# A third float64 load buffer with a changed scheduler, and five small edits, in an attention and two-MoE kernel

## The chip, the cores and the metric

The kernel runs on one core of one Trainium2 chip. The metric is the device time of one execution in microseconds, the median of several runs. The engines that matter are TensorE (PE, with its weight loads as PEld), VectorE (DVE), ScalarE (ACT) and the DMA queue that SyncE (SP) issues.

## The reference

A sigmoid attention over 4 batches and 12 heads of 448 tokens gives 1792 tokens of width 768. Two feed-forward layers follow, one after the other, each with a hidden width of 2048. The weights `w_in` and `w_out` come as float64 and are read as pairs of 32-bit words.

```python
scores = scale * np.matmul(q, k.transpose(0, 1, 3, 2)) - np.log(S)
attn = 1.0 / (1.0 + np.exp(-scores))
x = np.matmul(attn, v)                      # then (B*S, H*D) = (1792, 768)
# layer 1
r = np.maximum(x @ w_in, 0.0)
x = (s * (r * r) + b) @ w_out
# layer 2
h = x @ w_in
x = (np.maximum(h, 0.0) + alpha * np.minimum(h, 0.0)) @ w_out
```

## The kernel before

**Matmuls.** Every product of the two layers is made by the seven products M1 to M7 of the Strassen-Winograd scheme, and each operand is split in a high part (a CAST on ACT, L450) and a low part (a subtraction on DVE, L453). A term is three matmuls of 128x448: high times low (L547), high times high (L548), low times high (L549). The low part of a weight is thus needed at the third matmul. A "mp" is a pair of 128-row blocks of the hidden width; there are 8 in each phase, and one takes 63 matmuls, 9 for each of M1 to M7.

**Stages on PE.** Attention runs to 135.59 us of the span. Then come four pairs of phases: the tokens are halved, and each half goes through `w_in` and `w_out` of a layer. The first of them, `first_phase`, runs from 135.59 to 244.69 us and takes its weights straight from the buffers in which they are made; the later ones read them back from DRAM. The order of the products in `first_phase` is M1, M5, M6, M2, M4, M7, M3 (in mp7 M2 stands before M6). M1 and M2 share a bank of PSUM, M5 and M4 another, M6 and M7 a third: M2 can begin when M1's bank has been copied out (L558, ACT), M4 when M5's has been added (L568, DVE), M7 when M6's has been.

**Weights.** `quad` (L335) makes the operands of one mp: two loads of 768 KB on SP into the buffers `r640` and `r641` (shown as `r`; L328), for each of them a Prelu on ACT over the high words (L362), a TENSOR_SCALAR (L365) and a SCALAR_TENSOR_TENSOR (L370) on DVE, then four DVE subtractions or additions (L383), which leave seven blocks in `quada`, `quadb` or `quadc`. SP stores the blocks to DRAM (L402, L411). `first_phase` splits the blocks of `quadb` (even mp) and `quada` (odd mp) into the ring `rinq0` to `rinq3`: the first entry holds M1 and M5, the second M6 and M2, the third M4 and M7, the fourth M3. The buffers that `unit` (L426) loads weights back into, `raw0` and `raw1`, lie in the same memory as `quadb`.

**Results of M1 to M7.** They are gathered in `g`: M1 is copied (L558), M5 and M6 added (L568), M2 copied, M7 added and subtracted (L568, L576), M3 added. Relu (L594), Square (L629) and Identity with scale s and offset b (L632) then go over all four blocks of a mp, 1792 elements, on ACT.

**Order.** No engine chooses at run time. `Plan` collects every operation with an estimated duration and its dependencies; `place` puts, again and again, the operation that can start first (at equal starts the one with the least spare time, `late`) on its engine. That order is written out; each engine and the SP queue then run their rows strictly in this order. `order` repeats this ROUNDS times.

Of the kernel before, what the change touches and what calls it, by code (L numbers as in the profile page):

```python
# [16 lines left out]
P = 128  # L17
NWARM = 6
CELL = 64
QUEUES = {"SP": 0.07, "POOL": 1.0}  # L20
AHEAD = 1.0
ROUNDS = 3
SAFE = 0.0
PIPE = {"DVE": 0.08, "ACT": 0.09}
EARLY = 7
# [29 lines left out]
class Plan:  # L55
# [57 lines left out]
    def place(self, succ, late, pe):  # L113
        n = len(self.ops)
        share = self.shared()
        wrote, used = ([{} for _ in share] for _ in range(2))

        def behind(i, eng):

            x = 0.0  # L120
            for mine, of in zip(self.uses[i], (wrote, used)):
                for t in mine:
                    for o in share[t]:
                        for e, at in of[o].items():
                            if at > x and e != eng:
                                x = at
            return x
        left = [len(op[3]) for op in self.ops]
        est = [0.0] * n
        pe_at = 0  # L130
        open_ = {}
        for i in range(n):
            if left[i] == 0:
                open_.setdefault(self.ops[i][0], set()).add(i)
        free, done, at = {}, [], {}
        pipe = 0.0
        while len(done) < n:
            best = None
            for eng, cand in open_.items():
                if not cand:  # L140
                    continue
                f = free.get(eng, 0.0)
                if eng in QUEUES:
                    f = max(f, pipe - AHEAD)
                if eng == "PE":
                    i = pe[pe_at]
                    if i not in cand:
                        continue
                    est[i] = max(est[i], behind(i, eng))
                    pick = (max(f, est[i]), late[i], i)  # L150
                else:
                    while True:
# [3 lines left out]
                        if x <= pick[0]:  # L156
                            break
                        est[i] = x
                if best is None or pick < best[0]:
                    best = (pick, eng)  # L160
            (start, _, i), eng = best
            open_[eng].discard(i)
            if eng == "PE":
                pe_at += 1
            dur, lat = self.ops[i][1:3]
            if eng in QUEUES:
                free[eng] = start + QUEUES[eng]
                pipe = max(pipe, start) + dur
                end = pipe
            else:  # L170
                end = free[eng] = start + dur
            at[i] = start
            done.append(i)
            for k, mine in enumerate(self.uses[i]):
                for t in mine:
                    for of in (used, wrote)[: k + 1]:
# [33 lines left out]
def tile_kernel(  # L210
# [3 lines left out]
    vt: bass.AP,  # L214
    w_in1: bass.AP,
    w_out1: bass.AP,
    s: bass.AP,
    b: bass.AP,
    w_in2: bass.AP,
    w_out2: bass.AP,  # L220
    alpha: bass.AP,
    out: bass.AP,
):
    nc = tc.nc
# [16 lines left out]

    NSLOT = 37
    NRING, NRAW, NTMP = 3, 2, 7
    UNIT = 8 * P
    WQ = KH * P
    base0 = -(-nc.sbuf_base // (4 * CELL)) * CELL
# [16 lines left out]
    def own(name, n):  # L263
# [1 line left out]

    SLOTS = take(NSLOT * SLOT)
    RING0 = take(NRING * 2 * UNIT)
    PROD = take(8 * WQ + 7 * WQ)
    SPARE = take(NRAW * UNIT + 7 * WQ)
    RING = [tensor(f"ring{i}", RING0 + i * 2 * UNIT, 2 * UNIT, F32R) for i in range(NRING)]  # L270
    RING4 = [tensor(f"rinq{i}", RING0 + i * 4 * WQ, 4 * WQ, F32R) for i in range(4)]
# [8 lines left out]
        [(tensor("xraw12", MID + 2 * SLOT + XB, XB), 0, XB)],  # L280
        [(tensor("xraw13", MID + XB, S), 0, S), (tensor("xraw14", NEG.base, 2 * S), S, XB)],
    ]
    R64 = [tensor(f"r64{i}", PROD + 4 * WQ * i, 4 * WQ) for i in range(2)]
    QUADS = [
        tensor("quada", PROD + 8 * WQ, 7 * WQ),
        tensor("quadb", SPARE, 7 * WQ),
        tensor("quadc", NEG.base, 7 * WQ),
    ]
    TMP = [own(f"tmp{i}", S) for i in range(NTMP)]
    SMALL = take(CELL)  # L290
    BIAS, SC, BC, WARM, AL, NAL = (
        tensor(x, SMALL + at, n)
        for x, at, n in (
            ("bias", 0, 1), ("sc", 8, 1), ("bc", 16, 1), ("warm", 24, 1), ("al", 32, NFC), ("nal", 48, NFC)
        )
    )
    IDLE = tensor("idle", TMP[0].base, P)
# [14 lines left out]
        return 0.08 + 0.53e-3 * n  # L312

    def dma_t(n):
        return n * 4 * P / 345e3

    DMA_LAT = 2.2
    PE_LAT = 0.25
# [16 lines left out]
    def quad(m, kind, k, c, place=0):  # L335
# [11 lines left out]
        for row in range(2):  # L347
            src = w64[m, kind][2 * k + row]
            if kind == "out":
                src = src[:, 2 * c0 * P : 2 * c1 * P]  # L350
            r64 = R64[row]
            raw = sb(r64, 4 * n).bitcast(U32)
            load(raw, src.bitcast(U32), 4 * n, (), cells(r64, 4 * n), DMA_LAT + SAFE)
            v = raw.rearrange("p (b n t) -> p b n t", b=2, t=2)
# [57 lines left out]
            cells(QUAD, 7 * n), wrote, DMA_LAT,  # L412
        )

    n_unit = [0, 0]
    ring = {}

    def entry(chunks, ring_=RING):
# [158 lines left out]
            [("p", k)] + cells(other, S), cells(dst, S),  # L577
        )

    s_t, b_t = sb(SC, 1), sb(BC, 1)  # L580

    def nonlinear(m, par, mp, ps_, bank_=None):

# [39 lines left out]
    def scaled(m, par, mp, ps_):  # L623

        if m == 0:
            n = len(ps_) * S
            h = g_blocks(par, ps_, mp)
            c = [c for p in ps_ for c in cells(g_place(par, p, mp), S)]
            add("ACT", act_t(n), lambda: nc.scalar.activation(h, h, AF.Square), c, c)  # L629
            add(  # L630
                "ACT", act_t(n) + 0.19,
                lambda: nc.scalar.activation(h, h, AF.Identity, bias=b_t, scale=s_t),  # L632
                c + [("sc",)] + [("bc",)], c,
            )

    def first_phase(par):
        for mp in range(NMP):
            a, c, b, e = range(4 * (mp % 2), 4 * (mp % 2) + 4)
            have = []
            for x in ROWS[0][mp]:  # L640
# [307 lines left out]
    outs = [(0, "out", k, c) for c in range(len(CHUNKS)) for k in range(NDP)]  # L948
    quads += outs[:EARLY]
# [4 lines left out]
    def produce(n, both=False):  # L954
        for i in range(min(n, len(quads))):
            m, kind, k, c, *place = quads.pop(0)
            quad(m, kind, k, c, *(place or [2 * (i % 2) if both else 0]))

    for u in range(NU + 2):
        if u < NU:  # L960
# [19 lines left out]
    phases = [(0, 0), (0, 1), (1, 0), (1, 1)]  # L980
    for n, (m, g) in enumerate(phases):
        par = n % 2
        if n:
            in_phase(m, par)
        else:
# [64 lines left out]
```

## Time and profile before

| | us |
|---|---|
| median of 3 runs | 966.47 |
| lowest, highest of them | 966.35, 974.77 |
| the profiled execution | 970.06 |
| its span | 968.3 |
| PE busy | 954.7 |
| DVE busy | 729.6 |
| ACT busy | 653.1 |

The span is the time from the first to the last instruction of the profiled execution, 1.8 us less than its whole time. A busy PE counts a matmul to its modelled end, which overlaps the next one; so small gaps are found by counting matmuls in equal stretches.

### The profile page before, as it was taken

How to read it: one execution, taken by the hardware profiler on the slowest of the kernel's cores; microseconds unless marked ns; L12 is line 12 of the kernel's file. 1: busy time of each engine (PE TensorE's matmuls, PEld its weight loads, DVE VectorE, ACT ScalarE, POOL GpSimd, SP SyncE). 2: the span in 40 equal slices, each digit the busy share in tenths (PEclk: the TensorE clock that was granted, in tenths of full speed). 3: DMA queues.
4: the chain of work that ended last, by engine and by line, in shares of the span. 5: the costliest groups of instructions: out<-in, count | busy, mean ns of one | idle time of the engine just before them, and what ended most of it. 6: DMA issues, size and time to landing. Idle time of an engine off the chain costs nothing.

```text
span 968.3 us, 13904 instructions
## 1 busy us (share of the span) xinstructions
PE 954.7 (99%) x5424; PEld 810.4 (84%) x5424; DVE 729.6 (75%) x862; ACT 653.1 (67%) x793; POOL 0.2 (0%) x4
## 2 busy tenths in 40 slices
PE   9999999999999999999999999999999999999998
PEld 4343458988899999998999999999999999999997
DVE  2567648997995877788898969789968556699661
ACT  6989967788945546889946547677555466676451
POOL 0000000000000000000000000000000000000000
PEclk9999999999999999999999999999999999999999
DMA  8999978886663479997567787766444443333441
GB/s 277 343 329 330 348 253 283 291 279 251 213 207 109 145 237 333 311 334 264 190 185 225 252 333 274 247 215 217 148 134 150 138 117 107 103 109 119 133 146 66
DMA packets 81106, 211.68 MB, mean 219 GB/s; under 512 B 7184, under 2 KB 45840, under 8 KB 81040
## 3 DMA queue, kind: packets, MB, share of 16 engines
q1 hardware_dynamic: 81040, 210.80, 65.6%
q8 instruction: 42, 0.69, 0.3%
q14 instruction: 24, 0.20, 0.1%
HBM read 152.97 MB, written 57.80 MB: 218 GB/s over the span
## 4 chain that ended last, share of the span: by engine, by line
PE 67%; DVE 11%; DMA 10%; ACT 8%; issue 3%; SPq 0%; DVEq 0%; ACTq 0%
PE ps L547 20%; PE ps L548 20%; PE ps L549 20%; PE ps L857 4%; DMA w0out<-quada 4%; PE ps L895 3%; DMA r<-in_w_in 3%; DMA r<-in_w_out 3%; DVE ring L453 2%; DVE quada L383 1%; ACT g L629 1%; ACT g L632 1%; DVE quada L370 1%; DVE gb L453 1%; ACT ring L450 1%
## 5 line engine op out<-in xcount | busy, mean ns | idle before, releaser
L547 PE MATMUL ps<-gb,ring 128*128 128x448 f32 x672 | 245.8, 366 | 1.3 <-DVE gb L453 1.3
L549 PE MATMUL ps<-gb,ring 128*128 128x448 f32 x672 | 245.5, 365 | 0.6 <-DVE ring L453 0.6
L548 PE MATMUL ps<-gb,ring 128*128 128x448 f32 x672 | 245.4, 365 | 0.0
L453 DVE TENSOR_TENSOR ring<-raw,ring 128x1024 fp32r<-128x1024 f32 x147 | 179.5, 1221 | 76.5 <-ACT ring L450 76.5
L450 ACT CAST ring<-raw 128x1024 fp32r<-128x1024 f32 x147 | 154.1, 1048 | 100.3 <-PE ps L548 77.5
L547 PE MATMUL ps<-xo,ring 128*128 128x448 f32 x504 | 184.5, 366 | 0.4 <-DVE tmp L568 0.3
L549 PE MATMUL ps<-xo,ring 128*128 128x448 f32 x504 | 184.3, 366 | 0.0
L548 PE MATMUL ps<-xo,ring 128*128 128x448 f32 x504 | 184.3, 366 | 0.0
L547 PEld LDWEIGHTS ps<-gb,ring 128*128 128x128 f32 x672 | 126.2, 188 | 12.5 <-DVE gb L453 2.4
L549 PEld LDWEIGHTS ps<-gb,ring 128*128 128x128 f32 x672 | 126.2, 188 | 11.0 <-DVE ring L453 1.0
L548 PEld LDWEIGHTS ps<-gb,ring 128*128 128x128 f32 x672 | 126.2, 188 | 9.9
L453 DVE TENSOR_TENSOR gb<-g,gb 128x1344 fp32r<-128x1344 f32 (+1 forms) x84 | 116.7, 1399 | 15.2 <-ACT gb L450 13.6
L450 ACT CAST gb<-g 128x1344 fp32r<-128x1344 f32 (+1 forms) x84 | 99.5, 1193 | 25.2 <-PE ps L549 14.6
L547 PEld LDWEIGHTS ps<-xo,ring 128*128 128x128 f32 x504 | 94.6, 188 | 9.0 <-DVE tmp L568 0.6
L549 PEld LDWEIGHTS ps<-xo,ring 128*128 128x128 f32 x504 | 94.7, 188 | 7.8
L548 PEld LDWEIGHTS ps<-xo,ring 128*128 128x128 f32 x504 | 94.7, 188 | 7.8
L873 ACT ACTIVATE sg<-ps,bias 128x896 f32<-128x896 f32 x84 | 83.2, 1010 | 14.7 <-PE ps L857 14.1
L362 ACT ACTIVATE r<-r 128x768 f32<-128x768 f32 (+1 forms) x68 | 59.3, 873 | 42.1 <-DMA r<-in_w_out 23.0
L857 PE MATMUL ps<-kq 64*64 64x448 f32 x672 | 79.6, 548 | 2.8 <-ACT sg L873 2.7
L895 PE MATMUL ps<-sg,v 64*64 64x448 f32 x672 | 77.9, 536 | 0.0
L568 DVE TENSOR_TENSOR g<-ps,g 128x448 f32<-128x448 f32 x104 | 63.5, 620 | 17.3 <-ACT g L558 10.5
L547 PE MATMUL ps<-xo,rinq 128*128 128x448 f32 x168 | 62.5, 372 | 3.8 <-DVE g L568 2.2
(51 smaller groups left out, 994.5 us busy)
## 6 DMA issues: line engine op xcount, KB each, us to landing
r<-in_w_in SPq DMA_DIRECT2D x32, 768.0 KB, 5.9
raw<-w0out SPq DMA_DIRECT2D x42, 512.0 KB, 3.7
raw<-w1in SPq DMA_DIRECT2D x42, 512.0 KB, 3.6
raw<-w1out SPq DMA_DIRECT2D x42, 512.0 KB, 3.6
r<-in_w_out SPq DMA_DIRECT2D x24, 768.0 KB, 5.7
raw<-w0in SPq DMA_DIRECT2D x21, 512.0 KB, 5.7
kq<-in_qk SPq DMA_DIRECT2D x23, 448.0 KB, 5.4
w0out<-quada SPq DMA_DIRECT2D x6, 1344.0 KB, 7.9
```

The costliest lines, as they stand in the source:

```text
L362: nc.scalar.activation(hi, hi, AF.Prelu, scale=2.0**-112, alpha=-(2.0**32))
L370: nc.vector.scalar_tensor_tensor(out=u, in0=hi.bitcast(U32), scalar=3, in1=u, op0=ALU.logical_shift_left, op1=ALU.bitwise_or,)
L383: lambda: nc.vector.tensor_tensor(out=o_, in0=x_, in1=y_, op=op),
L450: add("ACT", act_t(n), lambda: nc.scalar.copy(h, x), cells(src, n), cells(hi, n))
L453: lambda: nc.vector.tensor_tensor(out=l, in0=x, in1=h.bitcast(F32), op=ALU.subtract),
L547: nc.tensor.matmul(d, wh_, ml_, start=first and k == 0, stop=False, **opt)
L548: nc.tensor.matmul(d, wh_, mh_, start=False, stop=False, **opt)
L549: nc.tensor.matmul(d, wl_, mh_, start=False, stop=last and k == n, **opt)
L568: lambda: nc.vector.tensor_tensor(out=d, in0=bank(k), in1=o, op=ALU.add),
L857: nc.tensor.matmul(ps[h * D : (h + 1) * D, k + j, :S], a.ap[rows, S + k0 : S + k0 + D], a.ap[rows, :S], start=True, stop=True,)
L873: lambda: nc.scalar.activation(o, i, AF.Sigmoid, bias=sb(BIAS, 1), scale=QKSCALE),
L895: nc.tensor.matmul(ps[j * D : (j + 1) * D, k + h, :S], va[keys, v : v + D], a.ap[keys, j * S : (j + 1) * S], start=first, stop=last,)
```

## The change

- The float64 loads rotate over three buffers, `r640`, `r641` and `r642`. Two buffers for the blocks are left, `quada` and `quadb`, and `quadb` no longer shares memory with `raw0` and `raw1`.
- The planner makes one round, takes a DMA for 319.4 GB/s instead of 345, and keeps a load on SP back (`POLITE`, `SLACK`, `ahead`) when an earlier operation of the program, not yet placed, uses the same memory under another name and is due before this load would have ended, with 4 us to spare.
- s, b and alpha come as one array `few` (128x18) in one load. The negated slopes, used by the second layer, are made in the second pair of phases instead of during attention.
- M2's bank is copied out with a Relu in the same instruction, and the later Relu goes over three blocks.
- The program is built with `dynamic_dma_scratch_size=1024`, and without this argument before.

```diff
+POLITE = ("SP",)
+SLACK = 4.0
-ROUNDS = 3
+ROUNDS = 1
+DMA_RATE = 319.4e3
...
+        def ahead(i, end):
+
+            for mine, of in zip(self.uses[i], open_uses[::-1]):
+                for t in mine:
+                    for o in share[t]:
+                        if any(j < i and late[j] < end for j in of[o]):
+                            return True
+            return False
...
+                        if eng in POLITE:
+                            dur, lat = self.ops[i][1:3]
+                            x = max(pick[0], pipe) if eng in QUEUES else pick[0]
+                            if ahead(i, x + dur + lat + SLACK):
+                                cand = cand - {i}
...
-            r64 = R64[row]
+            r64 = R64[n_unit[2] % NR64]
+            n_unit[2] += 1
...
-    R64 = [tensor(f"r64{i}", PROD + 4 * WQ * i, 4 * WQ) for i in range(2)]
+    R64 = [tensor(f"r64{i}", PROD + 4 * WQ * i, 4 * WQ) for i in range(NR64)]
     QUADS = [
-        tensor("quada", PROD + 8 * WQ, 7 * WQ),
-        tensor("quadb", SPARE, 7 * WQ),
-        tensor("quadc", NEG.base, 7 * WQ),
+        tensor("quada", PROD + 4 * NR64 * WQ, 7 * WQ),
+        tensor("quadb", NEG.base, 7 * WQ),
     ]
...
                 elif x == "M2":
-                    pcopy(p1, a)
+                    nonlinear(0, par, mp, [0], a)
                     if end:
-                        nonlinear(0, par, mp, [0])
                         scaled(0, par, mp, [0])
...
-            nonlinear(0, par, mp, [1] if end else [0, 1, 2, 3])
+            nonlinear(0, par, mp, [1] if end else [1, 2, 3])
...
-    load(s_t, s.to_broadcast([P, 1]), 1, (), [("sc",)])
-    load(b_t, b.to_broadcast([P, 1]), 1, (), [("bc",)])
-    load(sb(AL, NFC), alpha, NFC, (), [("al",)])
-    add(
-        "ACT", 0.22, lambda: nc.scalar.mul(sb(NAL, NFC), sb(AL, NFC), -1.0),
-        [("al",)], [("nal",)],
-    )
+    load(sb(FEW, 2 + NFC), few, 2 + NFC, (), [("few",)])
```

**How it moves instructions.** The order of the matmuls is the same. First the SP queue early in attention, before the change. `kq` and `v` are the attention's operands, `sc`, `bc` and `al` are s, b and alpha.

```order
L328 DMA r641_77<-in_w_in1 128x1536
L328 DMA sc_89<-in_s 128x1
L328 DMA v2_142<-in_vt 128x512
L328 DMA bc_90<-in_b 128x1
L328 DMA al_92<-in_alpha 128x16
L328 DMA r640_76<-in_w_out1 128x1536
```

The same queue at the same place, after it.

```order
L360 DMA r640_76<-in_w_in1 128x1536
L360 DMA v1_139<-in_vt 128x512
L360 DMA kq2_131<-in_qk 128x896
L360 DMA r642_78<-in_w_out1 128x1536
L360 DMA v2_140<-in_vt 128x512
L360 DMA r641_77<-in_w_in1 128x1536
```

The first load of `w_out` moves ahead of the second one of `w_in`, into the new buffer, and the three small loads are gone from here.

Next DVE at the end of mp2 in `first_phase`, before the change; `quada` holds the operands of mp3. The row `g0<-ps,g0` after the TENSOR_SCALAR is M7's addition.

```order
L383 TENSOR_TENSOR quada_78<-quada_78 128x384 x4
L453 TENSOR_TENSOR rinq0_63<-quada_78,rinq0_63 128x768
L453 TENSOR_TENSOR rinq1_64<-quada_78,rinq1_64 128x768
L365 TENSOR_SCALAR quadb_79<-r640_76 128x2x384
L568 TENSOR_TENSOR g0_114<-ps_95,g0_114 128x448
```

The same place after it; the first row is M7's addition.

```order
L601 TENSOR_TENSOR g0_112<-ps_93,g0_112 128x448
L416 TENSOR_TENSOR quada_79<-quada_79 128x384
L609 TENSOR_TENSOR g0_112<-g0_112,ps_93 128x448
L416 TENSOR_TENSOR quada_79<-quada_79 128x384
L486 TENSOR_TENSOR rinq2_65<-quada_79,rinq2_65 128x768
L486 TENSOR_TENSOR rinq0_63<-quada_79,rinq0_63 128x768
L486 TENSOR_TENSOR rinq1_64<-quada_79,rinq1_64 128x768
```

The low part of mp3's first ring entry, `rinq0`, moves from ahead of M7's addition to the fifth place behind it, after the one of the third entry.

Last the SP queue late in attention, before the change; mp0's stores `w0in<-quadb` stand far ahead of this, from the 24th row of the queue on.

```order
L328 DMA r_76<-in_w_out 128x1024
L328 DMA v_140<-in_vt 128x512
L328 DMA r_77<-in_w_out 128x1024
L411 DMA w0out<-quada 896x1x384
L728 DMA x_128<-tmp_81 128x448
L728 DMA x_128<-tmp_82 128x448
L328 DMA r_76<-in_w_in 128x1536
L328 DMA r_77<-in_w_in 128x1536
L411 DMA w0out<-quada 896x1x256
```

The same stretch after it; it begins a little earlier in attention.

```order
L435 DMA w0in<-quadb 128x4x384
L360 DMA r_76<-in_w_out 128x1024
L444 DMA w0out<-quada 896x1x384
L360 DMA r_77<-in_w_in 128x1536
L435 DMA w0in<-quadb 128x384 x3
L360 DMA few<-in_few 128x18
L760 DMA x_126<-tmp_86 128x448
L360 DMA r_78<-in_w_in 128x1536
L444 DMA w0out<-quada 896x1x256
L360 DMA r_76<-in_w_in 128x1536
L360 DMA raw_67<-w0out 128x1024
```

mp0's stores, mp1's two `w_in` loads, the first one of mp2 and the first `raw` load now stand in one stretch with the last `w_out` loads.

## Rows read from the trace of the kernel before

**Rows 1.** Stretches: busy us (x instructions) of PE, PEld, DVE, ACT, POOL; clock; DMA.

```profile
25.00:50.00 25.00, 23.01 (x248) 8.86 (x244) 14.13 (x20) 22.23 (x27) 0.00 (x0) 1.00 0.95 340
...
75.00:100.00 25.00, 24.17 (x256) 9.22 (x252) 19.23 (x25) 24.08 (x29) 0.00 (x0) 1.00 0.93 323
100.00:125.00 25.00, 25.00 (x272) 10.22 (x268) 12.93 (x20) 22.62 (x29) 0.00 (x0) 1.00 1.00 361
125.00:150.00 25.00, 25.00 (x187) 17.27 (x178) 15.88 (x28) 14.71 (x20) 0.00 (x0) 1.00 0.75 255
150.00:175.00 25.00, 24.05 (x119) 21.96 (x118) 21.79 (x39) 19.96 (x22) 0.00 (x0) 1.00 0.77 250
175.00:200.00 25.00, 24.27 (x120) 22.16 (x119) 21.89 (x39) 18.76 (x20) 0.00 (x0) 1.00 0.80 271
200.00:225.00 25.00, 22.73 (x111) 20.43 (x110) 20.58 (x34) 19.03 (x23) 0.00 (x0) 1.00 0.86 299
225.00:250.00 25.00, 24.26 (x110) 21.71 (x109) 23.59 (x29) 23.81 (x27) 0.00 (x0) 0.93 0.70 257
250.00:275.00 25.00, 25.00 (x125) 23.16 (x125) 25.00 (x24) 17.71 (x21) 0.00 (x0) 1.00 0.55 172
```

**Rows 2.** PE's waits: us in total, times, longest.

```profile
PE ps L857 <- ACT sg L873: 2.7, 3, 2.0
PE ps L547 <- DVE g L568: 2.2, 1, 2.2
PE ps L547 <- ACT g L558: 1.8, 3, 0.9
PE ps L547 <- DVE gb L453: 1.3, 3, 0.7
```

**Rows 3.** ACT's timeline in attention: start, us, instruction, idle before and its releaser.

```profile
23.57 0.21 ACT L944 ACTIVATE nal<-al 128x16 f32<-128x16 f32 x1 [0.82 <-DMA al<-in_alpha]
...
26.68 0.93 ACT L362 ACTIVATE r<-r 128x768 f32<-128x768 f32 x1 [1.58 <-DMA r<-in_w_out]
27.52 1.87 ACT L873 ACTIVATE sg<-ps,bias 128x896 f32<-128x896 f32 x2
```

**Rows 4.** The SP queue's timeline: start of the issue, us, transfer.

```profile
14.23 0.42 SPq L328 DMA_DIRECT2D r<-in_w_in  x1
...
19.01 0.38 SPq L328 DMA_DIRECT2D r<-in_w_out  x1
...
128.62 1.51 SPq L328 DMA_DIRECT2D r<-in_w_in  x2
...
218.93 0.32 SPq L328 DMA_DIRECT2D raw<-w0out  x1
```

**Rows 5.** ACT's timeline before mp2's M2.

```profile
164.85 0.89 ACT L362 ACTIVATE r<-r 128x768 f32<-128x768 f32 x1 [1.02 <-DMA r<-in_w_in]
165.65 1.68 ACT L594 ACTIVATE g<-g 128x1792 f32<-128x1792 f32 x1
167.24 0.51 ACT L558 COPY g<-ps 128x448 f32<-128x448 f32 x1
```

**Rows 6.** DVE's timeline before mp6's M4.

```profile
222.95 0.96 DVE L453 TENSOR_TENSOR rinq<-quadb,rinq 128x768 fp32r<-128x768 f32 x1 [3.61 <-DMA raw<-w0out]
```

**Rows 7.** PE's timeline after that wait.

```profile
224.49 0.47 PE L547 MATMUL ps<-xo,rinq 128*128 128x448 f32 x1 [2.16 <-DVE g L568]
...
226.13 0.58 PE L547 MATMUL ps<-xo,rinq 128*128 128x448 f32 x1
226.50 0.58 PE L548 MATMUL ps<-xo,rinq 128*128 128x448 f32 x1
```

**Rows 8.** DVE's timeline at the end of mp2.

```profile
171.00 2.33 DVE L383 TENSOR_TENSOR quada<-quada 128x384 f32<-128x384 f32 x4
173.25 1.82 DVE L453 TENSOR_TENSOR rinq<-quada,rinq 128x768 fp32r<-128x768 f32 x2
...
175.46 0.62 DVE L568 TENSOR_TENSOR g<-ps,g 128x448 f32<-128x448 f32 x1
```

More of the change, by code (lines that the diff above doesn't have):

```diff
@@ L127, in behind @@
             return x
+        open_uses = [[set() for _ in share] for _ in range(2)]
+        for i, mine in enumerate(self.uses):
+            for k in range(2):
+                for t in mine[k]:
+                    for of in open_uses[: k + 1]:
+                        of[t].add(i)
+        def ahead(i, end):
[5 more added lines that the diff above has]
+            return False
         left = [len(op[3]) for op in self.ops]
@@ L155, in place @@
                         x = behind(i, eng)
-                        if x <= pick[0]:
-                            break
-                        est[i] = x
+                        if x > pick[0]:
+                            est[i] = x
+                            continue
+                        if eng in POLITE:
[3 more added lines that the diff above has]
+                                cand = cand - {i}
+                                if not cand:
+                                    pick = None
+                                    break
+                                continue
+                        break
+                    if pick is None:
+                        continue
                 if best is None or pick < best[0]:
@@ L175, in place @@
                 for t in mine:
+                    for of in open_uses[: k + 1]:
+                        of[t].discard(i)
                     for of in (used, wrote)[: k + 1]:
@@ L216, in tile_kernel @@
     w_out1: bass.AP,
-    s: bass.AP,
-    b: bass.AP,
     w_in2: bass.AP,
     w_out2: bass.AP,
-    alpha: bass.AP,
+    few: bass.AP,
     out: bass.AP,
@@ L243, in tile_kernel @@
     NRING, NRAW, NTMP = 3, 2, 7
+    NR64 = 3
     UNIT = 8 * P
@@ L267, in tile_kernel @@
     RING0 = take(NRING * 2 * UNIT)
-    PROD = take(8 * WQ + 7 * WQ)
+    PROD = take((4 * NR64 + 7) * WQ)
     SPARE = take(NRAW * UNIT + 7 * WQ)
@@ L290, in tile_kernel @@
     SMALL = take(CELL)
-    BIAS, SC, BC, WARM, AL, NAL = (
+    BIAS, WARM, FEW, NAL = (
         tensor(x, SMALL + at, n)
         for x, at, n in (
-            ("bias", 0, 1), ("sc", 8, 1), ("bc", 16, 1), ("warm", 24, 1), ("al", 32, NFC), ("nal", 48, NFC)
+            ("bias", 0, 1), ("warm", 8, 1), ("few", 16, 2 + NFC), ("nal", 40, NFC)
         )
@@ L314, in dma_t @@
     def dma_t(n):
-        return n * 4 * P / 345e3
+        return n * 4 * P / DMA_RATE
     DMA_LAT = 2.2
@@ L413, in quad @@
         )
-    n_unit = [0, 0]
+    n_unit = [0, 0, 0]
     ring = {}
@@ L578, in psub @@
         )
-    s_t, b_t = sb(SC, 1), sb(BC, 1)
+    s_t, b_t, alpha_t = sb(FEW, 1), sb(FEW + 1, 1), sb(FEW + 2, NFC)
     def nonlinear(m, par, mp, ps_, bank_=None):
@@ L632, in scaled @@
                 lambda: nc.scalar.activation(h, h, AF.Identity, bias=b_t, scale=s_t),
-                c + [("sc",)] + [("bc",)], c,
+                c + [("few",)], c,
             )
@@ L956, in produce @@
             m, kind, k, c, *place = quads.pop(0)
-            quad(m, kind, k, c, *(place or [2 * (i % 2) if both else 0]))
+            quad(m, kind, k, c, *(place or [i % 2 if both else 0]))
     for u in range(NU + 2):
@@ L982, in tile_kernel @@
         par = n % 2
+        if n == 1:
+            add(
+                "ACT", 0.22, lambda: nc.scalar.mul(sb(NAL, NFC), alpha_t, -1.0),
+                [("few",)] + cells(X[par][0], S), [("nal",)],
+            )
         if n:
@@ L1032 @@
         "w_out1": w_out_tiles(moe_w_out),
-        "s": moe_s.reshape(1, 1),
-        "b": moe_b.reshape(1, 1),
         "w_in2": w_in_tiles(moe2_w_in),
         "w_out2": w_out_tiles(moe2_w_out),
-        "alpha": moe2_alpha.reshape(DFF // P, P).T,
+        "few": np.concatenate(
+            [np.broadcast_to(moe_s, (P, 1)), np.broadcast_to(moe_b, (P, 1)), moe2_alpha.reshape(DFF // P, P).T],
+            axis=1,
+        ),
     }
     arrays = {n: np.ascontiguousarray(a) for n, a in arrays.items()}
-    nc = bacc.Bacc("TRN2", target_bir_lowering=False, num_devices=1)
+    nc = bacc.Bacc("TRN2", target_bir_lowering=False, num_devices=1, dynamic_dma_scratch_size=1024)
     args = [
```

## The prediction

> **What bounds the kernel now.** I read the stretches first. In 250:275 PE issues 125 big matmuls in 25 us, 0.200 us each, at full clock and with no wait; in 100:125 it issues 272 of attention's smaller ones, 0.092 us each [rows 1]. Those are PE's full rates, and the change leaves PE's list as it is, so PE's gaps are all that it can win. Missing matmuls size them. Attention lacks 24 in 25:50 and 16 in 75:100, 40 x 0.092 = 3.7 us. The stretches from 150 to 250 lack 6, 5, 14 and 15, 40 x 0.200 = 8.0 us [rows 1]. A gap is longer than the wait that the profile names for it, because a busy matmul reaches into the idle time.
>
> Then PE's waits, for who ends each gap [rows 2]: the attention's sigmoid (2.7 us in 3 waits, one of 2.0), one addition by DVE (2.2), ACT's copies out of PSUM (1.8 in 3), DVE's low part of the activations (1.3 in 3). Last, each engine's timeline at these places:
>
> - *Near 26 us* ACT waits 0.82 us for alpha and then 1.58 us for the first `w_out` load, which SP issued at 19.01 and which releases the Prelu at 26.68; the next sigmoids stand behind both [rows 3, 4].
> - *Near 86 and 91 us* ACT is simply full, 24.08 of 25 us [rows 1].
> - *mp2 and mp4* lose about 1 us each at M2: its bank waits for the COPY of M1, which stands at 167.24 behind a Prelu that idled 1.02 us for its load and a Relu of 1.68 us [rows 5]. mp4 has the same pattern.
> - *mp6* loses most. A raw load issued at 218.93 [rows 4] holds DVE 3.61 us, and the addition that M4 waits for stands behind it [rows 6]: PE idles 2.16 us, and then matmuls start 0.37 us apart in place of 0.200 [rows 7]. The clock granted in 225:250 is 0.93 of full [rows 1], so PE ran there at the lower of its two levels (1.2 GHz) for some 10 matmuls, 10 x 0.17 = 1.7 us. Together about 4.0 us.
> - *At 248 us* the low part of the first activations of the next phase is late: the 0.7 us at the end of the last row of [rows 2], some 0.9 us of gap.
>
> **The change part by part.** *Attention.* Alpha's wait goes, as nothing on ACT needs it any more before the second pair of phases; s and b are first used in mp0. The `w_out` load moves from the sixth row of the shown piece of the queue to the fourth, past one v load, the second `w_in` load and the three small ones, and has a buffer of its own, so that it needs to wait for no Prelu and no DVE step on another buffer. It took 26.68 - 19.01 = 7.7 us from issue to use; the Prelu would have had to run 2.4 us (0.82 + 1.58) sooner. The second `w_in` load was issued at 14.23 [rows 4], and the `w_out` load now stands ahead of it, at least 19.01 - 14.23 = 4.8 us sooner, so this lead is there. I book the whole gap near 26 us, 24 x 0.092 = 2.2 us. Of the 1.5 us near 75 to 91, the part due to late loads should go and the part due to a full ACT stay: the Prelus and casts there are the same in number. I split it at 0.6 gained, between 0 and 1.5. Attention: 2.8 us, bounds 0 to 3.7.
>
> *mp6's wait.* `quadb` now has its own memory, and the first raw load stands in the queue late in attention. DVE has nothing to wait for there but the split of its own blocks, and the order puts mp6's first two low parts ahead of M7's addition of mp5. The wait and the slow clock behind it go: 4.0 us, bounds 2.3 (if another short wait takes its place and the clock holds) to 4.0.
>
> *mp2's and mp4's waits.* The new order puts ACT's copy of M1 in mp2 right behind a single Prelu and a cast, with the Square behind it. Also each mp has ACT's Relu over three blocks instead of four: the four cost 1.68 [rows 5], so about 1.25 by length, 0.4 us less in seven mp. M2's COPY becomes a Relu out of PSUM of the same shape, at the COPY's 0.51 [rows 5]. M2's own result is not read before the next mp, so the Relu itself is on no path. I book 1.7 of the two gaps of 1 us each, bounds 0.8 to 2.0.
>
> *mp3, a new wait.* This comes against the gains. mp3's first ring entry now stands on DVE as the fifth row behind M7's addition of mp2. PE needs 9 matmuls, 1.83 us, from M7's end to mp3's first one, and the low part at the third, so 2.2 us after M7's end. DVE needs, by busy times: the addition 0.62, a TENSOR_TENSOR on `quada` 0.58 (2.33 / 4), a subtraction from PSUM of the addition's length 0.62, another TENSOR_TENSOR 0.58, two low parts at 0.91 (1.82 / 2) [rows 8], 4.2 us. A step starts some 0.08 us before the one ahead of it ends (171.00 + 2.33 against 173.25 [rows 8]), five times 0.08 off, and I add 0.1 at each end for the signals between the engines, an estimate: 4.0 us. PE stalls 4.0 - 2.2 = 1.8 us. In the trace of before DVE did these parts ahead of M7's addition, at 173.25, and that addition at 175.46 hurt nobody [rows 8]. The clock is open: after the gaps of about 1 us PE kept its full clock (1.00 in 150:200), after the one of 2.3 it did not [rows 1, 7]. 1.8 lies half way. I take no drop; with one the cost is 1.8 + 1.7 = 3.5, the upper bound. The lower is 0, if mp2's end comes later than DVE for a reason that I don't see.
>
> *The edge at 248 us.* In the new order the third piece of the first activations comes as the fifth row from M7's addition in mp7: the addition, a difference of 1344, a subtraction, the low parts of 1024 and of 896. By the rows of mp2 scaled with the length, 0.62 + 1.59 + 0.62 + 1.21 + 1.06 = 5.1 us after M7 [rows 8]. It is needed at the third matmul behind M3 and two pieces of 9 matmuls, 3 x 1.83 + 0.4 = 5.9 us after M7. So most of the 0.9 goes: I book 0.7, bounds 0 to 0.9.
>
> *The rest.* Loads of the small arrays: two fewer issues on SP at some 0.4 us each, a queue that waits for DVE and ACT anyhow; nothing. The negation: 0.21 us on ACT [rows 3], now in the second pair of phases before M1's copies, where ACT has room as it has in 250:275, busy 17.7 of 25 us [rows 1]; nothing, and 0.2 if that cover were gone. The later phases have new rows too, and keep the rest of the third and fourth row of [rows 2], about 1 us of waits; I leave them as they are, within 1 us either way. DVE has 22 busy us in 25 in 150:200 and 23.6 in 225:250 [rows 1], so an order there has little room, and what it saves on one product it can owe on the next.
>
> Sum: 2.8 + 4.0 + 1.7 + 0.7 - 1.8 = 7.4 us. The profiled execution, 970.06 us, would become 962.7; it is 3.6 us over the median of the three runs, so the forecast for the median is 966.47 - 7.4 = **959.1 us**, 0.8% faster. A difference under 1% is about what a measurement of this kernel cannot tell from no change, and 1% is 9.7 us.
>
> **The rivals.** *All gaps go* (the mp3 stall is smaller, and ACT's dense stretch in attention eases with the shorter waits). Then 3.7 + 8.0 + 1 to 1.5 of the later gaps are won, less at most 1: 953 to 957 us, say 954.5. For it: 8.0 us lies in one phase, and its largest cause is out of the order. Against it: the row order at mp3 is fixed, and its steps have known times.
>
> *The waits only move* (the change does less than it says). One more stall like mp6's comes at a place where DVE waits for a load with an addition behind it, 4.0 us, and the clock falls at mp3, 1.7: 959.1 + 5.7 = 964.8 us. For it: in mp2 and mp4 a TENSOR_SCALAR into `quadb` now stands directly ahead of M6's addition, which M7 waits for. Against it: M6's addition has about 3.6 us of room there (one product of 1.83 for M2, one for M4), so only a load that is late by more than that costs anything.
>
> *The DMA becomes the bound at attention's end* (slower). Moved into the last stretch of attention are three `w_in` loads (3 x 0.79 MB), one raw load (0.52 MB) and mp0's stores (1.38 MB), 4.3 MB, or 11.8 us at the 361 GB/s of 100:125, where the DMA share is already 1.00 [rows 1]. In 125:135.6 a quarter is free, 2.6 us. So up to 9.2 us do not fit; before, the `w_in` loads were issued only at 128.62 [rows 4]. If the Prelus of these loads stand on ACT ahead of sigmoids, or the queue holds the last kq and v loads behind them, PE waits for all of it: 959.1 + 9.2 = 968.3 us, and up to 972 with a lower clock behind it. It decides from the point where the stall is over 7.4 us, so that most of the overflow must reach PE. Against it: these operands are not needed before mp1, near 148 us, and mp0's stores leave the early part of attention, which has 5% of its DMA time free besides (0.95 in 25:50).
>
> The Trainium skill (DMA: Bandwidth & Descriptors, Specifications) puts the limit of one core from HBM at about 358 GB/s, so that no third buffer could make more bytes arrive there; the 361 GB/s of 100:125 agrees with it [rows 1]. By that page, the last rival alone would set the end of attention, and the third buffer's 2.8 us would have to be struck from the sum, which would give 961.9.
>
> **How the numbers follow.** The forecast (957 to 962) has 0.50, all gaps gone 0.22, waits only moved (962 to 966.5) 0.16, the DMA bound 0.12. The range leaves out about a tenth at each end: below 954.0 only part of the second case, above 967.0 most of the last: 954 to 967 us. Faster by over 1% means under 956.8: the second case, and little of the first, 0.25. Slower by over 1% means over 976.1, which only the far end of the last case reaches, 0.03. Within 1%: 0.72.
>
> **What would show it.** In the profile of the changed kernel: 25:50 with 270 or more matmuls; no wait of DVE's low parts for a raw load in `first_phase`; a full clock at 225; and PE waiting some 1.8 us for the low part of a `rinq` (L486) near 172 us, a wait that the trace of before has nowhere. Attention should end near 132.8 and `first_phase` near 238.0. I would be wrong if the mp3 wait is missing or twice as long, if SP's order lets the `w_out` load land no earlier, or if 100:125 shows under 265 matmuls.

## The result and the profile after

The changed kernel takes 957.45 us, the median of 21 executions, against 972.46 for the kernel before beside it; the ratio is 0.9865, 95% interval [0.9837, 0.9893], so 1.35% faster. The ratio compares the means, without the one execution of 972.96 us, which lies over 1.5% above the changed kernel's fastest. The fastest executions are 956.25 and 966.35 us, 10.1 us apart. The profiled one took 956.32 us, 13.7 less than the profiled one of before. What may set the medians further apart than the fastest, 15.0 us, is told at the end (a rhythm of PE).

Where the time went, from the start of each phase's first matmul in the two traces, and to the start of the last one:

| stage | before, us | after, us | gained |
|---|---|---|---|
| attention, to its end | 135.59 | 130.87 | 4.72 |
| `first_phase` | 109.10 | 104.36 | 4.74 |
| first out phase | 103.23 | 102.14 | 1.09 |
| second pair of phases | 207.13 | 204.29 | 2.85 |
| the other four phases | 409.40 | 408.85 | 0.55 |

PE's waits in the changed kernel (us in total, times, longest; L580 and L582 are the matmuls L547 and L549 of before, L486 and L483 the splits, L957 the start):

```profile
PE ps L580 <- ACT rinq L483: 1.1, 1, 1.1
PE ps L957 <- DVE bias L963: 1.0, 1, 1.0
PE ps L582 <- DVE rinq L486: 0.4, 1, 0.4
PE ps L580 <- DVE gb L486: 0.2, 1, 0.2
```

All four lines of [rows 2] are gone but the last, which fell from 1.3 to 0.2. Two lines are new, and both are one place: mp3's first ring entry. The same stretches as in [rows 1], after:

```profile
25.00:50.00 25.00, 25.00 (x270) 11.81 (x266) 17.50 (x26) 23.29 (x29) 0.00 (x0) 1.00 0.95 328
...
75.00:100.00 25.00, 25.00 (x272) 9.95 (x268) 17.30 (x24) 24.90 (x31) 0.00 (x0) 1.00 0.91 311
100.00:125.00 25.00, 25.00 (x272) 10.19 (x268) 13.42 (x23) 21.19 (x27) 0.00 (x0) 1.00 0.97 334
125.00:150.00 25.00, 25.00 (x158) 19.88 (x151) 17.93 (x31) 12.54 (x18) 0.00 (x0) 1.00 0.92 310
150.00:175.00 25.00, 23.45 (x114) 21.07 (x114) 23.25 (x41) 21.25 (x25) 0.00 (x0) 1.00 0.93 312
175.00:200.00 25.00, 25.00 (x125) 23.16 (x125) 23.25 (x41) 20.77 (x24) 0.00 (x0) 1.00 0.99 335
200.00:225.00 25.00, 25.00 (x125) 23.17 (x124) 22.39 (x37) 20.45 (x23) 0.00 (x0) 1.00 0.91 317
225.00:250.00 25.00, 25.00 (x125) 23.01 (x124) 24.93 (x25) 24.90 (x28) 0.00 (x0) 1.00 0.64 235
```

Read the counts: attention is at 270 and 272 matmuls in 25 us, and from 175 on PE is full, 125 matmuls, the clock at 1.00 where it was 0.93. Only 150:175 lacks 11. In 100:125 the DMA share fell from 1.00 to 0.97, and in 150 to 225 it rose from between 0.77 and 0.86 to between 0.91 and 0.99: more is under way in `first_phase`, and no wait of PE names a load.

ACT's timeline at the place of [rows 3] (start, us, instruction, idle before):

```profile
21.22 0.91 ACT L395 ACTIVATE r<-r 128x768 f32<-128x768 f32 x1
22.01 1.01 ACT L905 ACTIVATE sg<-ps,bias 128x896 f32<-128x896 f32 x1
22.90 0.54 ACT L591 COPY xraw<-ps 128x448 f32<-128x448 f32 x1
23.32 1.04 ACT L905 ACTIVATE sg<-ps,bias 128x896 f32<-128x896 f32 x1
24.23 0.95 ACT L395 ACTIVATE r<-r 128x768 f32<-128x768 f32 x1
25.03 1.03 ACT L905 ACTIVATE sg<-ps,bias 128x896 f32<-128x896 f32 x1
```

No row has an idle time in brackets: ACT runs from one to the next. The first `w_out` load is issued at 13.11 and landed at 19.60 us, where before it landed at 26.60, and its Prelu, which ran at 26.68, runs at 21.22; the one at 24.23 is that of the second `w_in` load. The end of mp2, first DVE, then ACT, in the changed kernel:

```profile
167.66 0.62 DVE L601 TENSOR_TENSOR g<-ps,g 128x448 f32<-128x448 f32 x1
168.20 0.55 DVE L416 TENSOR_TENSOR quada<-quada 128x384 f32<-128x384 f32 x1
168.66 0.61 DVE L609 TENSOR_TENSOR g<-g,ps 128x448 f32<-128x448 f32 x1
169.20 0.55 DVE L416 TENSOR_TENSOR quada<-quada 128x384 f32<-128x384 f32 x1
169.79 2.69 DVE L486 TENSOR_TENSOR rinq<-quada,rinq 128x768 fp32r<-128x768 f32 x3
```

```profile
167.16 1.89 ACT L665 ACTIVATE g<-g,few 128x1792 f32<-128x1792 f32 x1
168.95 2.28 ACT L483 CAST rinq<-quada 128x768 fp32r<-128x768 f32 x3
```

These are the rows that the prediction put in a sum: M7's addition at 167.66, and the low part of mp3's first entry second of the three at 169.79, so done at 171.6. On ACT its high part is likewise second of three behind an Identity that ends at 169.05. PE's gap is 1.27 us for the high part and 0.61 for the low one, from the matmul starts.

### The profile page after: what moved, and what is told of

Read it like the earlier page. It is cut to its first block, busy times and chain, and to the rows that moved or that the text cites. A ratio compares the mean times of both kernels' runs of the same rounds, so it can differ in the third digit from the quotient of the medians.

```text
span 954.4 us, 13860 instructions
## 1 busy us (share of the span) xinstructions
PE 948.1 (99%) x5424; PEld 817.4 (86%) x5424; DVE 728.6 (76%) x862; ACT 651.0 (68%) x792; POOL 0.2 (0%) x4
## 4 chain that ended last, share of the span: by engine, by line
PE 94%; DVE 2%; ACT 1%; DMA 1%; issue 1%; SPq 0%; DVEq 0%; ACTq 0%
PE ps L582 27%; PE ps L580 27%; PE ps L581 27%; PE ps L889 7%; PE ps L927 7%; DMA w0in<-quadb 1%; DMA r<-in_w_in 1%; DVE rinq L486 0%; DVE gb L486 0%; PE ps L957 0%; ACT rinq L483 0%; ACT g L665 0%; DVE ring L486 0%; DVE g L601 0%; ACT neg L645 0%
## 5 line engine op out<-in xcount | busy, mean ns | idle before, releaser
L580 PE MATMUL ps<-gb,ring 128*128 128x448 f32 x672 | 245.5, 365 | 0.2 <-DVE gb L486 0.2
L582 PE MATMUL ps<-gb,ring 128*128 128x448 f32 x672 | 245.4, 365 | 0.0
L486 DVE TENSOR_TENSOR ring<-raw,ring 128x1024 fp32r<-128x1024 f32 x147 | 179.2, 1219 | 81.2 <-ACT ring L483 80.7
L483 ACT CAST ring<-raw 128x1024 fp32r<-128x1024 f32 x147 | 154.1, 1049 | 109.3 <-PE ps L581 97.6
L580 PE MATMUL ps<-xo,ring 128*128 128x448 f32 x504 | 184.1, 365 | 0.0
L582 PE MATMUL ps<-xo,ring 128*128 128x448 f32 x504 | 184.1, 365 | 0.0
L580 PEld LDWEIGHTS ps<-gb,ring 128*128 128x128 f32 x672 | 126.2, 188 | 10.6 <-DVE gb L486 0.6
L582 PEld LDWEIGHTS ps<-gb,ring 128*128 128x128 f32 x672 | 126.2, 188 | 10.0
L486 DVE TENSOR_TENSOR gb<-g,gb 128x1344 fp32r<-128x1344 f32 (+1 forms) x84 | 116.5, 1396 | 16.1 <-ACT gb L483 11.6
L483 ACT CAST gb<-g 128x1344 fp32r<-128x1344 f32 (+1 forms) x84 | 99.7, 1194 | 25.2 <-PE ps L582 15.6
L582 PEld LDWEIGHTS ps<-xo,ring 128*128 128x128 f32 x504 | 94.7, 188 | 7.5
L580 PEld LDWEIGHTS ps<-xo,ring 128*128 128x128 f32 x504 | 94.7, 188 | 7.5
L889 PE MATMUL ps<-kq 64*64 64x448 f32 x672 | 82.4, 539 | 0.0
L927 PE MATMUL ps<-sg,v 64*64 64x448 f32 x672 | 81.9, 536 | 0.0
L591 ACT COPY g<-ps 128x448 f32<-128x448 f32 x80 | 42.0, 529 | 40.9 <-PE ps L582 40.6
```

Source lines behind the costliest of these rows:

```text
L483: add("ACT", act_t(n), lambda: nc.scalar.copy(h, x), cells(src, n), cells(hi, n))
L486: lambda: nc.vector.tensor_tensor(out=l, in0=x, in1=h.bitcast(F32), op=ALU.subtract),
L580: nc.tensor.matmul(d, wh_, ml_, start=first and k == 0, stop=False, **opt)
L582: nc.tensor.matmul(d, wl_, mh_, start=False, stop=last and k == n, **opt)
L591: nc.scalar.copy(d, bank(k))
L889: nc.tensor.matmul(ps[h * D : (h + 1) * D, k + j, :S], a.ap[rows, S + k0 : S + k0 + D], a.ap[rows, :S], start=True, stop=True,)
```

## The experiments

All runs below, in one table: when attention ended, the length of `first_phase`, the seven later phases together, and the fastest and median execution with the number of executions. The stage lengths are of one profiled execution each; they need not be those of the median one (in new_buffers_old_planner it is the slowest, 974.88 us). In new_buffers_old_planner, two_load_buffers, quadb_apart_order_kept and changed_again the later phases are long mostly by the rhythm told at the end; in the kernel before and in small_loads_late_order_kept mostly by waits.

| kernel | attention | `first_phase` | later | fastest, median us |
|---|---|---|---|---|
| before | 135.59 | 109.10 | 719.76 | 966.35, 972.46 (21) |
| changed | 130.87 | 104.36 | 715.28 | 956.25, 957.45 (21) |
| small_edits_only | 138.34 | 115.06 | 716.51 | 975.53, 981.16 (4) |
| new_planner_old_buffers | 131.95 | 115.73 | 716.24 | 967.61, 971.19 (10) |
| new_buffers_old_planner | 131.55 | 110.40 | 727.33 | 960.35, 967.73 (10) |
| two_load_buffers | 131.45 | 116.62 | 723.36 | 968.79, 972.70 (10) |
| third_buffer_quadb_on_raw | 132.06 | 105.30 | 777.83 | 1020.80, 1022.13 (4) |
| no_load_held_back | 131.20 | 104.76 | 715.29 | 956.96, 957.99 (4) |
| quadb_apart_order_kept | 134.70 | 106.97 | 724.03 | 963.38, 970.23 (10) |
| negation_late_order_kept | 134.43 | 107.97 | 717.14 | 965.14 (1) |
| small_loads_late_order_kept | 135.44 | 110.80 | 719.16 | 971.01 (1) |
| mp3_low_part_first | 131.74 | 105.88 | 715.30 | 957.27, 969.98 (12) |
| short_matmul_at_each_phase | 131.63 | 104.20 | 715.91 | 957.62, 959.63 (4) |
| changed_again | 130.94 | 104.21 | 717.48 | 957.41, 958.02 (4) |

**My theory** was that each part of the change removes its own waits: the third buffer those of attention, `quadb`'s own memory the one of mp6, the new rows those of mp2 and mp4. **The rival**: the order alone makes the gain, or the small edits do.

**small_edits_only.** The kernel before with the one small load, the late negation and M2's Relu in its copy. Here and below, the edits are shortened: a list stands in one line, and where `quadc` comes back, the rule that chooses between the buffers for the blocks comes back with it.

```diff
# the changed kernel with
-NR64 = 3, QUADS = [quada, quadb at NEG.base]
+NR64 = 2, QUADS = [quada, quadb at SPARE, quadc at NEG.base]
-ROUNDS = 1, DMA_RATE = 319.4e3, POLITE = ("SP",)
+ROUNDS = 3, DMA_RATE = 345e3, POLITE = ()
```

> The kernel before with the small edits alone: s, b and alpha in one load, the negation later, M2's copy with its Relu; two load buffers, quadb in raw's memory, quadc, and the planner's old numbers. Theory (each part of the change removes its own waits): the edits alone win little, 0 to 3 us, fastest runs at 963 to 967 us, and the waits of mp6 in first_phase stay. Rival (the three small loads and alpha's wait were what mattered): 958 us or less.

Measured: slower than before, ratio 1.0118 [1.0033, 1.0203]. Both theories miss, and mp6's wait, which the first had staying, is not there. The edits give the planner other operations, and the rows that it then writes are worse:

```profile
PE ps L581 <- ACT g L592: 8.4, 4, 6.1
PE ps L890 <- ACT sg L906: 3.6, 4, 2.1
```

One COPY of M1 on ACT alone costs PE 6.1 us. What an edit is worth by its own operations (0.4 us of ACT in a mp) says nothing when every order around it is drawn again. This kernel also has the build argument `dynamic_dma_scratch_size`, as has every kernel made from the changed one; it was not tried by itself.

**new_planner_old_buffers, new_buffers_old_planner, two_load_buffers.** The two halves of the change, and the third load buffer by itself.

```diff
# new_planner_old_buffers: the changed kernel with
+NR64 = 2, QUADS = [quada, quadb at SPARE, quadc at NEG.base]
# new_buffers_old_planner: the changed kernel with
+ROUNDS = 3, DMA_RATE = 345e3, POLITE = ()
# two_load_buffers: the changed kernel with
+NR64 = 2
```

> The changed kernel with the old buffers (two load buffers, quadb in raw's memory, quadc beside it) and the new planner numbers and holding back of loads. Theory (the memory layout removes the largest wait, the third buffer attention's): 960 to 964 us, since holding loads back avoids only the wait on raw. Rival (the order alone makes the gain): 958 us or less.

> The changed kernel with the planner as it was (three rounds, 345 GB/s, no load held back), so new buffers and small edits alone. Theory: mp6's wait (4 us) and most of attention's (3.4) go with the buffers, whatever the order: 957 to 961 us. Rival (the order alone makes the gain): 964 us or more.

> The changed kernel with two float64 load buffers instead of three, all else as changed. Theory: attention loses its new lead, PE waits there for 2 to 4 us again (a stretch 25:50 with some 250 matmuls), and first_phase stays free of mp6's wait: 958 to 961 us. Rival (the third buffer buys nothing): 956 to 957.5 us, attention at 272 matmuls in 25 us.

Measured: ratios to before 1.0005 [0.9956, 1.0055], 0.9961 [0.9928, 0.9995] and 1.0017 [0.997, 1.0064]. Against the kernel before, the planner's half gives nothing, the buffers' half 0.4%, and without the third buffer nothing is left. But all three carry the small edits, so the kernel that differs from the halves in one thing alone is small_edits_only, which has neither. From its 1.0118 the planner gains 1.1%, the buffers 1.6% and both together 2.5%: over the whole time the halves add up, within the intervals. By stage, in one profile each, they do not. Attention ends at 138.3 us with neither half and at 130.9 to 132.0 with either or both; `first_phase` takes 115.1 us with neither, 115.7 with the planner's, 110.4 with the buffers' and 104.4 with both. Whether the small edits still cost anything beside both halves was not tried.

With the new buffers and the old planner mp6 has a wait even so, 2.3 us at 218 us, for ACT's copy of M1, which stands behind a Prelu that idled 4.88 us for its load:

```profile
PE ps L580 <- ACT g L591: 3.0, 2, 2.3
```

The third buffer does not act where I had it: attention ends at 131.5 us without it. With two load buffers it is `first_phase` that grows, from 104.4 to 116.6 us. PE's waits there:

```profile
PE ps L580 <- ACT rinq L483: 4.1, 3, 1.6
PE ps L582 <- DVE rinq L486: 3.6, 3, 1.2
```

Three times each, at mp1, mp3 and mp5: it is the wait that the changed kernel has at mp3 alone. DVE's timeline at the end of mp0 with two load buffers shows how it comes about:

```profile
139.35 1.82 DVE L403 SCALAR_TENSOR_TENSOR quada<-r,quada 128x768 uint32<-128x768 uint32 x2
142.69 0.62 DVE L601 TENSOR_TENSOR g<-ps,g 128x448 f32<-128x448 f32 x1 [1.52 <-PE ps L582]
143.24 0.55 DVE L416 TENSOR_TENSOR quada<-quada 128x384 f32<-128x384 f32 x1
143.70 0.61 DVE L609 TENSOR_TENSOR g<-g,ps 128x448 f32<-128x448 f32 x1
...
145.70 1.82 DVE L486 TENSOR_TENSOR rinq<-quada,rinq 128x768 fp32r<-128x768 f32 x2
```

DVE has all that it needs for `quada` at 141.2, and idles 1.52 us for M7, because M7's addition stands first in its row. Five rows stand between it and the low parts, much as at mp3, and PE's third matmul of mp1 starts at 147.58, when the second low part is done. With the third buffer it arises at mp3 alone. That the loads for mp1 and mp5, which have a free buffer earlier, are the reason is argued from the rows and was not tried by itself.

**third_buffer_quadb_on_raw.**

```diff
-        tensor("quadb", NEG.base, 7 * WQ),
+        tensor("quadb", SPARE, 7 * WQ),
```

> The changed kernel with quadb moved back into the memory of raw0 and raw1, three load buffers and the new planner kept. Theory (the third buffer and the new order are needed together, the shared memory costs only mp6's wait): first_phase without the waits for the low part at mp1 and mp5, mp6's wait back, 2 to 4 us more than changed: 958 to 961 us at best. Rival (quadb's own memory is what lets the order be good): first_phase as long as with two load buffers, about 116 us, 968 us.

Measured: 1022.13 us, ratio 1.051 [1.0473, 1.0547], but `first_phase` takes 105.30 us, within 1 us of the changed kernel. mp6's wait, which the theory had coming back, does not. So the shared memory costs nearly nothing there, and the loss is elsewhere:

```profile
PE ps L580 <- ACT ring L483: 57.6, 1, 57.6
```

It is one wait, at the first matmul of the second pair. With two buffers for the blocks, the second layer's blocks now go through `quadb` by turns, which `quadc` did before, and the loads back into raw stand behind all of them in the queue (`raw<-w0in` is issued at 393.14 us, with the matmul waiting from 340.8). By these rows, `quadb` needs its own memory because it took over `quadc`'s work.

**no_load_held_back.**

```diff
-POLITE = ("SP",)
+POLITE = ()
```

> The changed kernel without the rule that holds loads back; one round, 319.4 GB/s, three buffers, small edits. Theory (holding back only trims raw loads and the like): within 2 us of the changed kernel, 956 to 959 us at best, attention free of waits. Rival (it is what makes room for the loads in first_phase): first_phase over 110 us, 962 us or more.

Measured: 0.9846 [0.9798, 0.9894], fastest 956.96 us, stages within 0.4 us of the changed kernel. The holding back of loads, the largest piece of the diff, makes nothing of the gain here; what is left of the planner's part is its one round and its rate, which I did not take apart.

**quadb_apart_order_kept, negation_late_order_kept, small_loads_late_order_kept.** Here the order of before was written out as a list and kept, so that one thing changes and no row moves with it.

```diff
# quadb_apart_order_kept
-        tensor("quadb", SPARE, 7 * WQ),
+        tensor("quadb", NEG.base, 7 * WQ),
# negation_late_order_kept: the ACT operation L944 stands just ahead of its first reader
# small_loads_late_order_kept: the same, and the loads of sc, bc, al stand behind the third w_out load
```

> The kernel before with its order written out and kept, row for row, and only quadb moved out of raw's memory. Theory (the raw load's shared memory alone made mp6's wait): DVE's 3.6 us wait for the raw load, PE's wait of 2.2 us and the slow clock behind it go, 4 us, and the other gaps stay: 962 to 963 us at best. Rival (DVE is simply behind at mp6): another wait stands there, less than 1.5 us won.

> The kernel before with its order kept, and only the negation of the slopes moved from attention to the second layer. Theory (the sigmoid near 26 us waits for the w_out load last, and alpha's wait lies in its shadow): the wait of 2.0 us near 26 us stays within 0.2. Rival (the two waits add up): it falls by 0.8.

> As before this, and the three small loads also moved behind the third w_out load in the queue. Theory: the first w_out load is then issued when its buffer is free, 0.8 us sooner, and PE's wait near 26 us falls from 2.0 to about 1.2; the rest needs a buffer of its own. Rival (the small loads themselves slowed the large one down): it falls to under 0.5.

Measured, the first: 0.9948 [0.9912, 0.9984]. DVE no longer waits for the raw load at mp6:

```profile
219.69 0.95 DVE L521 TENSOR_TENSOR rinq<-quadb,rinq 128x768 fp32r<-128x768 f32 x1
220.56 0.62 DVE L636 TENSOR_TENSOR g<-ps,g 128x448 f32<-128x448 f32 x1
```

The row of [rows 6] stands here without its 3.61 us, PE has no gap at mp6 and no slow clock, and `first_phase` is 2.1 us shorter. The other gaps stay or grow (1.69 us at mp2, against 1.11), by some 2 us together, and take back half of the 4 us that mp6 loses in the trace of before. So the cause of mp6's wait is shown, but the time that it gives back is half of what I booked. In the two other runs with before's order (below) mp6's wait of 2.0 and 1.7 us is there, and the clock does not fall behind it. The 1.7 us of slow clock that I read off [rows 7] came in one execution of the three that have the wait.

The two others settle nothing. PE's gap near 26 us, 2.2 us in the profile of before, is 0.5 and none; but it is also 0.7 in the run in which only `quadb` moved, so the landing of that one load differs by over 1 us from execution to execution: with the same queue, 7.6, 6.2 and 5.9 us after its issue, and 5.4 with the small loads moved. Attention ended at 134.4 to 135.6 us in all four: what is not waited for there is waited for later.

**mp3_low_part_first.** The changed kernel with a few rows put in another order.

```diff
 # ACT:  ... Square of mp1
-Identity of mp1, CAST rinq2, CAST rinq0, CAST rinq1
+CAST rinq0, CAST rinq1, Identity of mp1, CAST rinq2
 # DVE:
-TT, M7's addition, TT, subtraction, TT, low rinq2, low rinq0, low rinq1
+TT x3, low rinq0, M7's addition, subtraction, low rinq2, low rinq1
```

> The changed kernel with one change of order: for mp3, the high and low part of the first ring entry stand ahead of mp1's Identity and the third entry on ACT, and ahead of M7's addition of mp2 on DVE. Theory (the wait at mp3 is nothing but this order): PE's wait of 1.1 and 0.4 us there goes, 1.9 us with what follows it, span 952.5, fastest runs at 954.4. Rival (DVE or ACT is behind as a whole): the wait moves to another place in mp3 or mp4 and the time stays at 956.3.

Measured: 0.9905 [0.986, 0.9949], fastest 957.27; `first_phase` 105.88 us, longer by 1.5, of which 0.7 is a slow rhythm (told at the end) in its first 175 matmuls, before the moved rows. The wait at mp3 falls from 1.9 to 0.26 us, but DVE and ACT now owe the work that was put off:

```profile
170.56 0.96 DVE L498 TENSOR_TENSOR rinq<-quada,rinq 128x768 fp32r<-128x768 f32 x1 [0.31 <-ACT rinq L495]
...
173.80 1.83 DVE L498 TENSOR_TENSOR rinq<-quada,rinq 128x768 fp32r<-128x768 f32 x2 [1.10 <-ACT rinq L495]
```

Gaps of 0.36, 0.51, 0.67 and 0.39 us follow within the next 62 us, so that the gaps sum to 2.2 us where the changed kernel lost 1.9 at mp3. My theory falls here: the order sets where the wait lies, but the amount is owed by ACT and DVE, busy 21 and 23 of 25 us at that place.

**short_matmul_at_each_phase, changed_again.**

```diff
# in the first group of each of the seven later phases
+            if extra:
...
+                nc.tensor.matmul(ps[:, dst_bank, S : S + 64], sb(wh, P), sb(mh, 64), start=True, stop=True)
```

> The changed kernel with one extra matmul of 64 columns, into unused columns of PSUM, ahead of each of the seven later phases. Theory (PE falls in one of two steady rhythms, 0.2027 or 0.2067 us a matmul, at each break in its row, and a break of any kind draws anew): the executions spread over levels of 2.0 us above 956.7, most with one to three slow phases, 957 to 963 us, and none near 970. Rival (only a wait breaks the rhythm, or the level belongs to the execution): as the changed kernel, nearly all at 956 to 958 and some near 970.

> The changed kernel itself, beside the others on one chip. Theory: fastest at 956 to 957.5 us; where an execution is slower, it is by a stretch at 0.2067 us a matmul from the last wait in first_phase (near 171 us) to the next one (near 850 us), up to 13.5 us. Rival: levels between these, without a wait that begins them.

Measured: 957.62, 957.97, 961.28 and 961.51 us with the short matmuls; 957.41, 957.53, 958.51 and 972.45 without. The first lie within the range that the theory gave and the 972 appears only in the second, but four executions each cannot tell that from chance, and in the one profile with the short matmuls none of the seven changed PE's rhythm. The profile of changed_again, the 958.51 us one, shows the rhythm itself (PE's count is the first in brackets):

```profile
825.00:850.00 25.00, 25.00 (x125) 23.05 (x123) 22.69 (x24) 19.87 (x28) 0.00 (x0) 1.00 0.32 105
850.00:875.00 25.00, 24.78 (x121) 22.33 (x120) 23.41 (x25) 16.22 (x23) 0.00 (x0) 1.00 0.35 115
875.00:900.00 25.00, 25.00 (x123) 22.71 (x122) 21.46 (x19) 12.46 (x12) 0.00 (x0) 1.00 0.38 124
900.00:925.00 25.00, 25.00 (x123) 22.71 (x122) 13.74 (x13) 13.58 (x16) 0.00 (x0) 1.00 0.40 124
```

PE has no idle time from 875 on and a clock of 1.00, yet issues 123 matmuls where it issued 125. The change of pace comes with the one wait of 0.4 us near 850, and costs that phase 2.0 us (104.39 against 102.42).

## Why the prediction was right

The forecast was 959.1 us, in a range of 954 to 967, and 0.8% faster; measured are 957.45 and 1.35%. That the time came out within 1.7 us is in part luck. The 7.4 us were taken off 966.47, the median of three executions; over 21 it is 972.46, 6.0 us more. And the sum was too small: the profiled executions lie 13.7 us apart, the medians 15.0. The two errors nearly cancel. The places and their causes were mostly right, the sizes not; against the stage lengths, attention was booked too low by 1.9 us, `first_phase` by 0.8, the edge by 0.4 and the later phases by 3.4. Point by point:

- *Attention, booked 2.8 of 3.7.* 4.72 us came. Of these 1.4 are the start: PE's first 24 score matmuls took from 3.68 to 7.23 us in the profile of before and from 3.67 to 5.86 after, with nothing of the change in between. In before four of them start every 0.73 us or so until 6.7 us, in the changed kernel every 0.37 us from 4.4 us on; in the other profiles the 24th starts anywhere from 5.84 to 7.08. The rest, 3.3, is nearly the whole 3.7, so I was too careful about ACT's dense stretch: it is busy 24.90 of 25 us there and PE still loses only 0.2 us. The cause was wrong: with two load buffers attention ends just as early, so its gain needs either half of the change and not the third buffer. The 2.2 us booked near 26 us are those of one execution; in two others with the same queue that gap is 0.5 and 0.7 us, and other gaps are longer.
- *mp6, booked 4.0.* The wait is gone, and moving `quadb` alone shows why. In most executions it is worth about 2 us, as the slow clock behind it came in one of three.
- *mp2 and mp4, booked 1.7.* Both are gone, 2.0 us.
- *mp3, booked as a cost of 1.8.* It came as worked out, at 169.1 us, with 1.27 + 0.61 us and the full clock kept. DVE's rows took 4.0 us from M7's addition to the low part, as in the sum, and they end the second and last of the two waits. ACT's rows, which I had not named, end the first.
- *The edge at 248 us, booked 0.7.* The first out phase gained 1.09: its gap of 0.9 and what follows a gap.
- *The rest, booked 0.* This term was mis-sized. The second pair of phases and the one after it gained 3.4 us: gaps of some 2.4 (near 404, 452, 454 and 559 us in the trace of before), and 0.9 of slow rhythm from 404 to 452. I had seen these waits in [rows 2] and left them, though the new rows cover these phases too.
- *The rivals.* "All gaps go" came closest: nearly all but mp3's went. The DMA did not become the bound: its share in 100:125 is 0.97, and PE waits for no load in attention. The Trainium skill (DMA: Bandwidth & Descriptors, Specifications) puts the limit of one core from HBM at about 358 GB/s. The traces lie near it, at 334 and 335 GB/s with shares of 0.97 and 0.99 here and at 361 before [rows 1].

In `first_phase` the new buffers and the planner's numbers are worth much more together than apart, as the table shows in one profile each. Which of the planner's numbers does it stays open.

## What to carry to other kernels

When a table or planner writes the order, price a part against the kernel that differs in that part alone. The halves here looked worth 0 and 0.4% against the kernel before, and 1.1 and 1.6% against the one with neither, because edits of small worth had drawn a worse order. Keep the order fixed to learn what one buffer or load costs. A late low part that is repaired by hand on engines with 2 to 4 us of 25 to spare comes back elsewhere; count what they owe before moving rows.

## What was not expected of the hardware

PE's dense rows run in one of two steady rhythms at a granted clock of 1.00. In most traces matmul starts are 203, 202, 203, 199 and 207 ns apart, by turns, 0.2027 us on the mean; in the other rhythm 207, 207 and 206 ns, 0.2067 us. A phase of 504 matmuls takes 102.14 us in the one and 104.16 in the other. In the profiles the rhythm changed only at a break in PE's row and held until the next one (the smallest, in mp3_low_part_first at 228 us, is a start a few ns late). In that of before it was slow from the wait at 404 us to the one at 452, in new_buffers_old_planner from 241 us, where a slow clock ends, to 869 us, six phases, 12 us. That kernel's stretches:

```profile
250.00:275.00 25.00, 25.00 (x122) 22.71 (x121) 23.86 (x22) 16.53 (x19) 0.00 (x0) 1.00 0.38 125
...
875.00:900.00 25.00, 25.00 (x125) 23.15 (x125) 23.60 (x23) 16.53 (x20) 0.00 (x0) 1.00 0.35 115
```

A wait can thus cost more than its length: it may leave PE 2% slower until the next one. The length of the break does not decide it: one of 0.57 to 0.58 us from start to start, near 850 to 870 us, left PE fast in the changed kernel and slow in changed_again and two_load_buffers. This would explain the levels of the times. mp3_low_part_first has five executions at 957.3 to 961.9 us and seven at 970.0 to 972.8; from its last wait in `first_phase` (233 us) to its next (852) lie 3050 matmuls, which at 0.0040 us more make 12.2 us. The changed kernel has few breaks, with none between 171 and 850 us, and 16 of its 21 executions are within 3.2 us of its fastest. The kernel before has breaks in six of the eight phases, and 6 of its 21 are within 1 us of its fastest and the rest 4 to 13 us above. That the longer times come from this is argued from such sums, as no execution of the changed kernel at 970 us was profiled. Its slowest, 972.96 us, is 16.7 us above its fastest, and all 4032 matmuls of the eight phases at the slow pace would make 16.1. What picks the rhythm is open.
